# Value loads on another engine's queue, weight loads one piece less ahead, and a later start of the norm, in an attention and two-layer gated-FFN kernel

## The chip, the cores and the metric

One core of a Trainium2 chip runs the whole program. The metric is device time in microseconds (us), the median of several executions; the profile is one further execution with the hardware profiler on. Engines are named as the profile names them: PE is TensorE (PEld its weight loads), DVE VectorE, ACT ScalarE, POOL GpSimd, SP SyncE, which here only issues transfers ("SPq" in the trace).

## The reference

```python
def reference(q, k, v, w_a, w_b, w_out1, w_gate, w_val, w_out2, rms_g):
    # q, k, v: 4 batches, 8 heads, 576 tokens, 64 wide
    scores = q @ k.transpose(0, 1, 3, 2) / 8.0
    scores = where(block_of(i) >= block_of(j), scores, -1e9)     # blocks of 64 tokens
    attn = softmax(scores)
    x = (attn @ v).transpose(0, 2, 1, 3).reshape(2304, 512)
    x = ((x @ w_a) * (x @ w_b)) @ w_out1                          # 512 -> 1536 -> 512
    xn = x / sqrt(mean(x * x) + 1e-6) * rms_g
    g, val = xn @ w_gate, xn @ w_val
    return (g * sigmoid(g) * val) @ w_out2
```

## The kernel before, in words

The program has three parts that overlap. **Attention** (`attention`, L307 on) goes over 16 pairs of heads, numbered m = 0 to 15, four pairs to a batch. A pair is done in two halves of its rows (`part` 0 and 1), and step u = 2m + part scores one half, transposes the half before it and multiplies the half before that with the values. **Layer one** (`moe1`) follows batch by batch, in blocks of 512 or 1,024 tokens with 512 or 256 columns to a matmul. While it runs on one block, the attention of the next batch is woven in between its matmuls, so PE has work of two kinds in its queue. **Layer two** (`moe2`) has three blocks of 768 tokens and saves one product in eight twice over by sums of operands (seven products for eight, P1 to P7), 384 columns to a matmul. Nearly every operand of the layers is split in two, a rounded high part (made by ACT or DVE) and the rest (by DVE or POOL), and a product is three matmuls.

The kernel is written in an order, and a scheduler then sorts each engine's queue by its own estimates. Each engine then works off its queue strictly in order: an instruction that waits holds up all that stands behind it. Before the change every transfer is issued from SP's queue.

What the change touches:

- **The values.** `load_v(m)` (L387) fetches the values of pair m. The four pairs of the first batch (`WHOLE = 1`) are used whole. From pair 4 on they are split: `make_vv(m)` (L422) makes the high part at L114 and the rest at L429, both on POOL, from a raw tile `vr`. Pair 4 has a raw tile of its own; pairs 5 to 15 take turns in the two `vr` buffers, which pairs 0, 2 and 3 used before them, whole. So a load of the raw values waits until a former pair has read its buffer for the last time: for pair 5 these are the value matmuls of pair 2 on PE (L548), for most later pairs the split two pairs ahead on POOL (L429). Before, `load(m)`, called two pairs ahead, calls `load_v(m)`; each pair is two transfers of 160 KB, one for each head, at L403.
- **The weights.** Weights come as 8-byte numbers in 72 pieces of 512 KB. `prepare()` (L192) first lets `stage_loads` issue the loads of some pieces ahead (at L190), then decodes one piece: two ACT passes (L146, L149), a DVE shift (L152) and a POOL addition (L153), after which the piece is split (L111, L121) and written out again (L227). Five landing places go round (`LANDING = 5`: three in the tile `ld`, two in `st`). The load of a piece waits until the piece that lay in its place is decoded. Before, loads run up to five pieces ahead of the one decoded, for the first half of the pieces (layer one).
- **The norm.** `normed` (L1002) fetches the next block's tokens from DRAM (L1006), squares and sums them (L1009 and L1011 on ACT, L1012 on DVE), splits the sum, adds over partitions with two matmuls per half (L1023, L1024), takes the root and scales (L1026 to L1044), and `sums_of` makes four differences of operands (L959). `before_fc` (L1091) takes one step of it at each of the 24 calls in a block of layer two. Before, the first step is taken at the call with `fc` = 1.

At the border of the layers the tokens of the block after next have just been written to DRAM (L1088), and the norm's fetch of them waits for that write.

Of the kernel before, what the change touches and what calls it, by code (L numbers as in the profile page):

```python
# [16 lines left out]
P = 128  # L17
# [34 lines left out]
def tile_attention_moe_moe(  # L52
# [121 lines left out]
    def stage_loads(n):  # L174
        while len(staged) + prepared[0] < min(n, len(w_pieces)):
            i = len(staged) + prepared[0]
            layer, kind, f, y = w_pieces[i]
            if layer == 0 and i % LANDING < LANDING - 2:
                if not landing:
                    landing.append(stage.tile([P, LANDING - 2, 4 * P], I64, tag="bg", name="ld", bufs=1))  # L180
                st = landing[0][:, i % LANDING]
            else:
                st = stage.tile([P, 4 * P], I64, tag="st", name="st", bufs=2)
            if kind == "o" and layer == 1:

                for dm in range(KC):
                    z, o = divmod(dm * TF + f % TF, KC)
                    sp.dma_start(out=st[:, dm * P:dm * P + P], in_=w_o[1][f // TF, z, :, o * P:o * P + P])
            else:
                sp.dma_start(out=st, in_=(w_ab if kind == "ab" else w_o)[layer][f, y])  # L190
            staged[i] = st

    def prepare():

        i = prepared[0]
        if i >= len(w_pieces):
            return
        stage_loads(min(i + min(2 + i, LANDING), max(len(w_pieces) // 2, i + 2)))
        layer, kind, f, y = w_pieces[i]
        w = 4 * P  # L200
        if layer == 0:
            if y == 0:
                if kind == "ab":
                    wtiles["ab", f] = wab.tile([P, 4, KC * P], F32R, tag="ab", name="ab")
                else:
                    wtiles["o", f] = wop.tile([P, 2, TF * DM], F32R, tag="o", name="o")
            t = wtiles[kind, f]
            dst = t[:, 2 * y:2 * y + 2, :] if kind == "ab" else t[:, :, y * w:(y + 1) * w]
        else:
            if f % 2 == 0:  # L210
                quarters["src"] = stage.tile([P, 8, 2 * P], F32, tag="src", name="src", bufs=1)
            src = quarters["src"]
            if kind == "ab":
                at = (0, 6)[f % 2]
                place = src[:, at:at + 2, :]
            else:
                place = src[:, f % 2:f % 2 + 7:6, :]
            decode(staged.pop(i), place)
            prepared[0] += 1
            if f % 2 == 1:  # L220
                combine(wc_dram[f // 2][y] if kind == "ab" else wco_dram[f // 2], src)
            return
        x = decode(staged.pop(i)).rearrange("p a b -> p (a b)")
        prepared[0] += 1
        split(dst[:, 0, :], dst[:, 1, :], x, act, eng[W_LO[i % len(W_LO)]], "act")
        if y == (1 if kind == "ab" else TF - 1):
            sp.dma_start(out=wab_dram[f] if kind == "ab" else wo_dram[f], in_=t.bitcast(F32))  # L227
# [82 lines left out]
    def attention(pools, x_of, done):  # L310
# [44 lines left out]
        def load(m):  # L355
            if m >= NP:
                return
            b, h = divmod(m, H // 2)
            if single(m):
                t = k_raw[m] = ap2.tile([P, 2, S], F32, tag="kr", name="kr", bufs=1)  # L360
                for y in range(2):
                    rows = slice(y * D, y * D + D)
                    sp.dma_start(out=t[rows], in_=k[b, h].rearrange("(t d) s -> d t s", t=2))
                if m == FIRST_SINGLE:
                    load_q(m)
                load_v(m)
                return
            if m == 0:
                t = k_raw[m] = stage.tile([P, 8, 2 * P], F32, tag="src", name="src", bufs=1).rearrange(
                    "p a b -> p (a b)"  # L370
                )[:, 0:S]
            else:
                t = k_raw[m] = ap2.tile([P, 2, S], F32, tag="kr", name="kr", bufs=1)[:, 0]
                sp.dma_start(out=t, in_=k[b, h])
            for n0, n1 in ((0, FIRST), (FIRST, NQ)) if m == 0 else ((0, NQ),):
                cols = slice(n0 * Q, n1 * Q)
                if m == 0:
                    sp.dma_start(out=t[:, cols], in_=k[b, h][:, cols])
                for hh in range(2):
                    sp.dma_start(  # L380
                        out=qz[m % 2][hh * D:hh * D + D, n0:n1, hh, :],
                        in_=q[b, 2 * h + hh][:, cols].rearrange("d (n q) -> d n q", q=Q),
                    )
            if m > 1:
                load_v(m)

        def load_v(m):  # L387
            b, h = divmod(m, H // 2)
            if b < WHOLE:
                if m == 1:  # L390
                    t = ap2.tile([P, 2, NTILE, P], F32, tag="vv", name="vr")
                    t = vv[m] = t[:, 0].rearrange("p n (h d) -> p n h d", h=2)
                else:
                    t = vv[m] = ap2.tile([P, NTILE, 2, D], F32, tag="vr", name="vr")
                for hh in range(2):
                    sp.dma_start(out=t[:, :, hh], in_=v[b, 2 * h + hh])
                return
            if m == WHOLE * (H // 2):
                t = v_raw[m] = ap2.tile([P, 2, NTILE, P], F32, tag="vv", name="vr")[:, :, :, 0:D]
            else:  # L400
                t = v_raw[m] = ap2.tile([P, 2, NTILE, D], F32, tag="vr", name="vr")
            for hh in range(2):
                sp.dma_start(out=t[:, hh], in_=v[b, 2 * h + hh])  # L403

        def make_k(m):
            if m >= NP:
# [208 lines left out]
        for u in range(2 * NP + 2):  # L615
            m, part = divmod(u, 2)
            if u >= 2:
                yield from (whole_values if (u - 2) // H < WHOLE else values)(u - 2)
            sc = list(SCORED[part]) if m < NP else []
            ct = p_transposes(u - 1) if 1 <= u <= 2 * NP else iter(())  # L620
            if sc:
                yield score(m, sc.pop(0))
                if len(sc) > 2:
                    yield score(m, sc.pop(0))
                if part == 0:
                    make_vv(m)
                    make_q(m, 1)
                else:
                    make_k(m + 1)
                    if m + 1 > FIRST_SINGLE:  # L630
                        make_q(m + 1, 0)
            alive = True
            while sc or alive:
                c = next(ct, None) if alive else None
                if c is None:
                    alive = False
                else:
                    yield c
                if sc:
                    yield score(m, sc.pop(0))  # L640
            if m < NP and part == 1:
                if m + 1 == FIRST_SINGLE:
                    make_q(m + 1, 0)
                load(m + 2)
# [414 lines left out]
    for at, (layer, t0, n_tok, parts) in enumerate(blocks):  # L1059
# [32 lines left out]
        def before_fc(fc, n_tiles=n_tiles, at=at, layer=layer, following=following, norm=norm, got=got):  # L1092
            if at == 0:
                if fc > 0:
                    for _ in range(TF):
                        if prepared[0] < len(w_pieces) // 2:
                            prepare()
            elif layer == 0:
                if fc % TF == 0:
                    fetch_o(fc // TF)  # L1100
                if fc + 2 < FC:
                    fetch_ab(fc + 2)
                n = sum(BACKGROUND[:at]) + min(BACKGROUND[at], BACKGROUND[at] * (fc + 1) // (FC - 3))
                while prepared[0] < len(w_pieces) // 2 + n:
                    prepare()
                if prepared[0] == len(w_pieces) and not rings:
                    staging.close()
                    rings.append(ctx.enter_context(tc.tile_pool(name="ring", bufs=RING, side="right")))
                    fetch_to(RING - 1)
            if following and following[0] == 0 and fc + 2 >= FC:  # L1110
                fetch_ab(fc + 2 - FC)
            if fc > 0:
                for _ in range(FC * 2 // n_tiles):
                    if layer == 0 and len(got.get("x") or ()) == len(EARLY):
                        break
                    got["x"] = next(norm, None) or got.get("x")
# [100 lines left out]
```

## Time and profile before

| what | value |
|---|---|
| median of 3 runs | 1054.71 us (1053.46 to 1057.16) |
| the profiled execution: its time | 1053.99 us |
| its span on the core | 1052.0 us |
| granted TensorE clock, mean over the span | 0.998 |
| busy: PE, PEld | 1037.8 us (99%), 934.4 us (89%) |
| busy: DVE, ACT, POOL | 702.6 us, 619.0 us, 423.5 us |
| transfers | 281.25 MB, all but 1.08 MB of it from SP's queue |

A line of a timeline gives the start of an instruction and its duration in us, then engine, line, operation, tiles and shapes; in brackets the time for which the engine stood idle before it, and the instruction that ended that. A line of a waits view gives the instruction that waited, the one it waited for, and total us, number of times, longest us. The chain is the work that ended last, followed back in time: start, us, and what. PEclk is the granted TensorE clock as a share of full speed.

### The profile page before, as it was taken

What the parts mean: (1) busy time and instruction counts of PE and PEld (TensorE: products, weight loads), DVE (VectorE), ACT (ScalarE), POOL (GpSimd) and SP (SyncE); (2) the same over time, 40 slices, a digit from 0 to 9 for tenths busy, and PEclk for the clock granted to TensorE, in tenths of its full rate; (3) what the DMA queues carried; (4) which work ended last, traced back from release to release, by engine and by line L of the source; (5) the groups of instructions that cost most, each with busy time, mean ns of one, the idle gap of its engine ahead of it and who ended that gap; (6) DMA issues with size and microseconds to landing.
All of it is one profiled execution on the core that took longest, in us unless ns stands there. A gap on an engine that the chain in (4) does not pass through costs nothing.

```text
span 1052.0 us, 16959 instructions
## 1 busy us (share of the span) xinstructions
PE 1037.8 (99%) x5676; PEld 934.4 (89%) x5676; DVE 702.6 (67%) x1371; ACT 619.0 (59%) x1376; POOL 423.5 (40%) x448
## 2 busy tenths in 40 slices
PE   9989999999999999999999999999999999999998
PEld 6768877899998888888888888999999999999998
DVE  5546767677766777676687734784876838666285
ACT  7868968667656766556544323653656536355362
POOL 5855766546564655455554501120221202212020
PEclk9999999999999999999999999999999999999999
DMA  9865978889997765788989665787789888887883
GB/s 242 232 202 194 294 258 300 313 270 290 347 371 261 270 223 210 288 330 313 340 312 349 255 225 181 216 284 258 242 301 302 275 268 251 294 265 240 266 247 116
DMA packets 116380, 281.25 MB, mean 267 GB/s; under 512 B 27971, under 2 KB 40771, under 8 KB 105798
## 3 DMA queue, kind: packets, MB, share of 16 engines
q1 hardware_dynamic: 116294, 280.18, 79.8%
q8 instruction: 45, 0.74, 0.3%
q14 instruction: 41, 0.34, 0.1%
HBM read 218.77 MB, written 61.36 MB: 266 GB/s over the span
## 4 chain that ended last, share of the span: by engine, by line
PE 85%; ACT 4%; DMA 4%; DVE 2%; POOL 2%; SPq 1%; issue 1%; POOLq 0%; ACTq 0%
PE mm L735 25%; PE mm L766 12%; PE mm L707 8%; PE mm L708 8%; PE mm L709 8%; PE mm L667 4%; PE mm L668 4%; PE mm L669 4%; PE t L592 3%; PE t L523 3%; PE s L465 3%; PE t L548 1%; DMA st<-in_w_o_dram 1%; POOL x L153 1%; PE s L457 1%
## 5 line engine op out<-in xcount | busy, mean ns | idle before, releaser
L708 PE MATMUL mm<-xl,ab 128*128 128x512 f32 (+1 forms) x480 | 180.8, 377 | 0.0
L707 PE MATMUL mm<-xh,ab 128*128 128x512 f32 (+1 forms) x480 | 179.8, 377 | 0.0
L709 PE MATMUL mm<-xh,ab 128*128 128x512 f32 (+1 forms) x480 | 179.4, 374 | 0.0
L735 PE MATMUL mm<-hT,w 128*128 128x384 f32 x576 | 165.5, 337 | 1.3 <-ACT mm L743 1.3
L121 POOL TENSOR_TENSOR hl<-g,hh 128x384 fp32r<-128x384 f32 x36 | 42.7, 1186 | 298.7 <-ACT hh L111 298.7
L735 PE MATMUL mm<-hB,w 128*128 128x384 f32 x432 | 125.9, 336 | 0.0
L766 PE MATMUL mm<-hh,w 128*128 128x384 f32 x504 | 125.2, 336 | 0.0
L743 ACT ACTIVATE mm<-mm 128x384 f32<-128x384 f32 x144 | 66.8, 474 | 75.5 <-PE mm L735 39.3
L735 PEld LDWEIGHTS mm<-hT,w 128*128 128x128 f32 x576 | 105.9, 188 | 2.7 <-ACT mm L743 2.4
L709 PEld LDWEIGHTS mm<-xh,ab 128*128 128x128 f32 x480 | 90.5, 189 | 15.2 <-issue 0.5
L707 PEld LDWEIGHTS mm<-xh,ab 128*128 128x128 f32 x480 | 90.4, 188 | 15.1 <-issue 0.2
L708 PEld LDWEIGHTS mm<-xl,ab 128*128 128x128 f32 x480 | 90.5, 189 | 14.8 <-issue 0.2
L498 POOL TENSOR_SCALAR pp<-pp,st 128x256 f32<-128x256 f32 (+4 forms) x144 | 83.3, 592 | 50.0 <-DVE st L495 35.5
L735 PE MATMUL mm<-lT,w 128*128 128x384 f32 x288 | 96.9, 337 | 0.0
L486 ACT ACTIVATE pp<-s,st 128x288 f32<-128x288 f32 (+8 forms) x142 | 72.0, 510 | 33.0 <-DVE st L480 16.2
L766 PEld LDWEIGHTS mm<-hh,w 128*128 128x128 f32 x504 | 90.6, 188 | 0.3 <-ACT mm L743 0.3
L766 PE MATMUL mm<-hl,w 128*128 128x384 f32 x252 | 81.4, 336 | 0.0
L735 PEld LDWEIGHTS mm<-hB,w 128*128 128x128 f32 x432 | 79.5, 188 | 0.0
L667 PE MATMUL mm<-hh,o 128*128 128x512 f32 (+1 forms) x208 | 77.8, 375 | 1.2 <-DVE acc L677 0.7
L153 POOL TENSOR_TENSOR src<-src,st 128x512 uint32<-128x512 uint32 x36 | 47.8, 1328 | 74.0 <-DVE src L152 74.0
L668 PE MATMUL mm<-hh,o 128*128 128x512 f32 (+1 forms) x208 | 77.4, 373 | 0.0
L669 PE MATMUL mm<-hl,o 128*128 128x512 f32 (+1 forms) x208 | 75.3, 370 | 0.4 <-DVE hl L121 0.4
(161 smaller groups left out, 2453.4 us busy)
## 6 DMA issues: line engine op xcount, KB each, us to landing
w<-wc SPq DMA_DIRECT2D x252, 256.0 KB, 3.5
ab<-wab SPq DMA_DIRECT2D x36, 1024.0 KB, 7.9
w<-wco SPq DMA_DIRECT2D x126, 256.0 KB, 3.3
wc<-bg SPq DMA_DIRECT2D x12, 1792.0 KB, 8.3
o<-wo SPq DMA_DIRECT2D x12, 1536.0 KB, 8.0
st<-in_w_ab_dram SPq DMA_DIRECT2D x34, 512.0 KB, 5.7
wab<-ab SPq DMA_DIRECT2D x12, 1024.0 KB, 5.9
wco<-bg SPq DMA_DIRECT2D x6, 1792.0 KB, 6.6
```

Source lines behind the costliest of these rows:

```text
L153: pool.tensor_tensor(x, x, lo, ALU.add)
L486: act.activation(pi[:, a:z], pss[x][:, 0:z - a], AF.Exp, bias=s[:, b:b + 1], scale=1.0, accum_out=t3[:, b, x:x + 1],)
L498: pool.tensor_scalar(t, t, s[:, y:y + 1], 1.0, ALU.mult, ALU.mult)
L667: pe.matmul(ps[:, 0:n], wh, hh, start=(y == 0), stop=False)
L668: pe.matmul(ps[:, 0:n], wl, hh, start=False, stop=False)
L669: pe.matmul(ps[:, 0:n], wh, hl, start=False, stop=(y == TF - 1))
L707: pe.matmul(ps[:, 0:n], wh[:, a:z], xhc, start=(c == 0), stop=False)
L708: pe.matmul(ps[:, 0:n], wh[:, a:z], xlc, start=False, stop=False)
L709: pe.matmul(ps[:, 0:n], wl[:, a:z], xhc, start=False, stop=(c == KC - 1))
L735: pe.matmul(ps, lhs, rhs[:, c, :], start=(start and c == 0 and y == 0), stop=(c == 1 and y == 2), skip_group_check=not start,)
L743: act.activation(to, ps, AF.Copy)
L766: pe.matmul(banks[m], lhs, rhs, start=(start and f == group[0] and y == 0), stop=(f == group[-1] and y == 2), skip_group_check=not start,)
```

## The change

Values of pairs 5 to 15 are loaded by one transfer of 320 KB each from POOL's queue, and the load for pair m + 1 is written directly behind the split of pair m. Weight loads run four pieces ahead where they ran five ahead. In layer two the norm's first step is taken at the call with `fc` = 3; layer one's calls (`layer` = 0) are as they were.

```diff
@@ prepare
-        stage_loads(min(i + min(2 + i, LANDING), max(len(w_pieces) // 2, i + 2)))
+        stage_loads(min(i + min(2 + i, LANDING - 1), max(len(w_pieces) // 2, i + 2)))
@@ load
                 if m == FIRST_SINGLE:
                     load_q(m)
-                load_v(m)
                 return
...
-            if m > 1:
+            if 1 < m <= WHOLE * (H // 2):
                 load_v(m)
@@ load_v
             if m == WHOLE * (H // 2):
                 t = v_raw[m] = ap2.tile([P, 2, NTILE, P], F32, tag="vv", name="vr")[:, :, :, 0:D]
-            else:
-                t = v_raw[m] = ap2.tile([P, 2, NTILE, D], F32, tag="vr", name="vr")
-            for hh in range(2):
-                sp.dma_start(out=t[:, hh], in_=v[b, 2 * h + hh])
+                for hh in range(2):
+                    sp.dma_start(out=t[:, hh], in_=v[b, 2 * h + hh])
+                return
+            t = v_raw[m] = ap2.tile([P, 2, NTILE, D], F32, tag="vr", name="vr")
+            pool.dma_start(out=t, in_=v[b, 2 * h:2 * h + 2].rearrange("t p n d -> p t n d"))
@@ attention, part 0 of pair m
                     make_vv(m)
+                    if WHOLE * (H // 2) <= m < NP - 1:
+                        load_v(m + 1)
                     make_q(m, 1)
@@ before_fc
-            if fc > 0:
+            if fc > 2 * layer:
```

How this moves instructions in the queues, at the three places the prediction speaks of. (Line numbers of the changed kernel are higher by one or two from `make_vv` on.)

**POOL, around the split of pair 5.** L153 decodes weights, L498 scales a tile `pp` of softmax rows, L114 and L429 split the values of pair 5, and L121 is a split of weights. Before:

```order
L153 TENSOR_TENSOR x<-x,ld 128x512
L498 TENSOR_SCALAR pp_158<-pp_158,st 128x576
L114 TENSOR_SCALAR vv<-vr 128x10x64
L429 TENSOR_TENSOR vv<-vr,vv 128x10x64
L153 TENSOR_TENSOR x<-x,ld 128x512
L498 TENSOR_SCALAR pp_156<-pp_156,st 128x448
L498 TENSOR_SCALAR pp_157<-pp_157,st 128x512
L121 TENSOR_TENSOR o<-x,o 128x512
```

Now:

```order
L153 TENSOR_TENSOR x<-x,ld 128x512
L498 TENSOR_SCALAR pp_158<-pp_158,st 128x576
L403 DMA vr<-in_v_dram 128x2x320
L114 TENSOR_SCALAR vv<-vr 128x10x64
L429 TENSOR_TENSOR vv<-vr,vv 128x10x64
L153 TENSOR_TENSOR x<-x,ld 128x512
L498 TENSOR_SCALAR pp_156<-pp_156,st 128x448
L498 TENSOR_SCALAR pp_157<-pp_157,st 128x512
L403 DMA vr<-in_v_dram 128x2x320
L121 TENSOR_TENSOR o<-x,o 128x512
```

The load of pair 5 (the first L403) stands right in front of the split that needs it, and the load of pair 6 four rows behind that split; on SP the two pairs of L403 rows are gone and its other rows stand in the order they had.

**ACT, at the border of the layers.** L111 makes high parts of layer two's first operands, L1009 and L1011 are the norm's squares, L743 and L862 copy products out of PSUM for PE. Before:

```order
L111 ACTIVATE hT_6896<-T_6522 128x768
L1009 ACTIVATE sq<-xf 128x768
L1011 ACTIVATE y<-xf 128x768
L743 ACTIVATE mm<-mm 128x384
L1011 ACTIVATE y<-xf 128x768
L862 ACTIVATE p_7042<-mm 128x384
L743 ACTIVATE mm<-mm 128x384 x2
L1011 ACTIVATE y<-xf 128x768
L819 ACT_TABLE_LOAD
```

Now (L1013 was L1011, L745 was L743, L864 was L862, L821 was L819):

```order
L111 ACTIVATE hT_6885<-T_6511 128x768
L1013 ACTIVATE y<-xf 128x768
L745 ACTIVATE mm<-mm 128x384
L864 ACTIVATE p_7031<-mm 128x384
L745 ACTIVATE mm<-mm 128x384 x2
L821 ACT_TABLE_LOAD
```

One of the two squares that stood in front of the first PSUM copy is still there; the other, and two more, have moved some ten rows back.

**ACT, in the later attention of layer one.** L486 are exponentials of scores, L146 and L149 decode weights, and L111 splits them. Before:

```order
L146 ACTIVATE ld<-ld 128x512
L149 ACTIVATE a<-ld 128x512
L486 ACTIVATE pp_154,st<-s,st 128x320
L111 ACTIVATE ab<-x 128x512
L486 ACTIVATE pp_155,st<-s,st 128x384
L597 ACTIVATE xf<-t 64x192
L111 ACTIVATE o<-x 128x512
```

Now:

```order
L146 ACTIVATE ld<-ld 128x512
L111 ACTIVATE ab<-x 128x512
L486 ACTIVATE pp_154,st<-s,st 128x320
L149 ACTIVATE a<-ld 128x512
L486 ACTIVATE pp_155,st<-s,st 128x384
L111 ACTIVATE ab<-x 128x512
L597 ACTIVATE xf<-t 64x192 x2
```

The second exponential stands ahead of the split of weights that was between the two; swaps of this kind fill the stretch on ACT, DVE, POOL and PE.

## Rows read from the trace of the kernel before

**Rows 1.** The page's 40 slices: PE's clock, in tenths.

```profile
PEclk9999999999999999999999999999999999999999
```

**Rows 2.** Waits of PE from 50 us to the end: seven of all eight rows.

```profile
PE t L523 <- POOL pp L498: 3.2, 4, 2.0
PE mm L735 <- ACT mm L743: 1.3, 1, 1.3
PE s L457 <- ACT pp L486: 1.1, 1, 1.1
PE mm L667 <- DVE acc L677: 0.7, 2, 0.4
PE t L592 <- DVE pl L529: 0.5, 1, 0.5
PE mm L667 <- ACT hh L111: 0.5, 1, 0.5
...
PE mm L669 <- DVE hl L121: 0.4, 1, 0.4
```

**Rows 3.** Timeline of POOL, 56 to 66 us.

```profile
56.31 0.74 POOL L498 TENSOR_SCALAR pp<-pp,st 128x576 f32<-128x576 f32 x1
61.36 0.72 POOL L114 TENSOR_SCALAR vv<-vr 128x640 fp32r<-128x640 f32 x1 [4.31 <-DMA vr<-in_v_dram]
62.17 1.55 POOL L429 TENSOR_TENSOR vv<-vr,vv 128x640 fp32r<-128x640 f32 x1
```

**Rows 4.** Timeline of PE, 56 us: the value matmuls of pair 2.

```profile
56.10 0.39 PE L548 MATMUL t<-pw,vr 128*128 128x128 f32 x2
```

**Rows 5.** Timeline of SP's queue, 56 us: the row before the load.

```profile
56.35 0.33 SPq L190 DMA_DIRECT2D ld<-in_w_o_dram  x1
```

**Rows 6.** The chain: the load of pair 5, eleven transposes soon after, and eleven later.

```profile
57.21 4.00 DMA vr<-in_v_dram
...
67.05 2.35 PE t L523 x11
...
196.61 1.20 PE t L523 x11
```

**Rows 7.** Windows: stretch, PE, PEld, DVE, ACT, POOL, then PEclk, DMA share, GB/s.

```profile
67.00:68.00 1.00, 1.00 (x7) 1.00 (x6) 0.42 (x1) 0.28 (x1) 0.47 (x1) 0.50 0.84 344
...
250.00:275.00 25.00, 25.00 (x208) 24.83 (x207) 21.08 (x59) 19.44 (x52) 17.25 (x21) 1.00 1.01 345
```

**Rows 8.** Line L403, all 24 transfers: from issue to landing, us.

```profile
DMA to landing us min/median/max: 2.2/3.4/9.4
```

**Rows 9.** Timeline of POOL: what follows the places of the next five value loads.

```profile
69.36 1.51 POOL L498 TENSOR_SCALAR pp<-pp,st 128x64 f32<-128x64 f32 x4 [1.89 <-DVE st L495]
77.43 1.29 POOL L121 TENSOR_TENSOR xl<-xf,xh 128x512 fp32r<-128x512 f32 x1 [2.87 <-DVE xh L113]
111.23 1.31 POOL L153 TENSOR_TENSOR x<-x,ld 128x512 uint32<-128x512 uint32 x1 [0.37 <-DVE x L152]
146.91 0.75 POOL L498 TENSOR_SCALAR pp<-pp,st 128x576 f32<-128x576 f32 x1 [3.01 <-ACT ph L525]
182.92 0.75 POOL L498 TENSOR_SCALAR pp<-pp,st 128x576 f32<-128x576 f32 x1 [1.10 <-DVE st L495]
```

**Rows 10.** Waits of PE, 110 to 215 us: two of four; the others stand above.

```profile
PE t L523 <- POOL pp L498: 1.2, 3, 0.6
...
PE mm L667 <- DVE acc L677: 0.3, 1, 0.3
```

**Rows 11.** The chain at the border of the layers.

```profile
644.02 7.70 DMA xf<-x_dram
...
651.74 0.02 ACT sq L1009
...
652.49 0.82 ACT y L1011
```

**Rows 12.** Timeline of DVE, 59 us: the last of four operations that follow each other.

```profile
59.29 0.69 DVE L121 TENSOR_TENSOR xl<-xf,xh 128x512 fp32r<-128x512 f32 x1 [0.33 <-ACT xh L111]
```

## The prediction

> **What bounds the kernel now.** I read the page's slices first: PE's clock is at its full level in every slice [rows 1], and the table above has PE busy for 99% of the span. So PE is the bound, and a change can give back only what PE loses. The waits of PE come second [rows 2]. From 50 us to the end they are 3.2 + 1.3 + 1.1 + 0.7 + 0.5 + 0.5 + 0.4 + 0.4 = 8.1 us (the row left out is one of the two of 0.4). Beside the waits there is one stretch near 67 us at half clock, granted 0.50 [rows 7]: eleven transposes took 2.35 us there, against 1.20 later [rows 6], so 1.15 lost. That is 9.3 us of 1,054 in all; no version of this change can bring 1%.
>
> The two largest waits lie where the diff works, so I read their surroundings third. The first is the 2.0 us at L523, which waits for a `pp` of POOL's. POOL was late because it had stood idle for 4.31 us before the split of pair 5's values, L114 at 61.36, until their load landed [rows 3]. That load runs on the chain from 57.21 to 61.21 [rows 6]. PE idles, and right behind it comes the half clock. The second is the 1.3 us at L735 at the border of the layers: ACT first makes two squares of the norm and only then the copy of PSUM for which PE waits [rows 2, 11].
>
> **The change part by part.**
>
> *A, the load of pair 5.* It leaves SP's queue and stands on POOL's between the scale L498 and the split. Does it start earlier? Its buffer is free when PE is through with pair 2's values, at 56.10 + 0.39 = 56.49 [rows 4]; SP was at another load until 56.35 + 0.33 = 56.68 [rows 5], so SP lost nothing by standing elsewhere. POOL comes to the load when L498 ends, at 56.31 + 0.74 = 57.05 [rows 3], later than SP. The buffer is free by then, so the load adds no wait on a semaphore; but the next row on POOL needs its data, so all of its landing is again POOL's idle time. No row of this kernel shows a load issued by POOL. For POOL's hold I have below the 0.33 of an issue on SP [rows 5], above the 1.55 of L429, POOL's longer pass over the same tile [rows 3]. I take 1.14, the mean of its two passes over that tile, 0.72 and 1.55, since the tile is the same, though a descriptor is no pass. For landing I keep the 4.00 of this load. Then L114 begins at 57.05 + 1.14 + 4.00 = 62.19 where it began at 61.36: **+0.83**. From below: hold 0 and the shortest landing of this line, 2.2 [rows 8], give 59.25, 2.11 earlier; PE's wait of 2.0 goes with it. From above: hold 1.55 and the longest landing, 9.4, give 68.0, 6.6 later.
>
> *B, the other ten loads.* Each holds POOL for 1.14. The next five stand ahead of idle times of POOL of 1.89, 2.87, 0.37, 3.01 and 1.10 [rows 9], so four of the five are covered to within 0.04 and one runs over by 0.77, in front of a decoding addition, L153, not of something PE waits for. The last ones fall where PE works through without a gap, 25.00 of 25 [rows 7]. I take **0**; without that cover, +0.8. They land in time: the places are 8 to 36 us apart, the median landing 3.4 [rows 8, 9].
>
> *C, SP without the loads, and four pieces ahead.* SP's remaining rows stand in the order they had, and a piece's load starts when its place is decoded, which the count of pieces ahead doesn't alter: **0**. If the count did bite, PE would wait for weights, of which there is no row now [rows 2].
>
> *D, the re-sorted stretch from 110 to 215 us.* PE waits 1.2 + 0.3 [rows 10] and, in the same stretch, 1.1 and 0.5 of the rows above (L457 and L667 behind `hh`) [rows 2]: 3.1 in all. It can lose at most that and, by the same measure, gain as much again. The one readable move is that exponentials pass ahead of splits of weights, and L457 waits for an exponential; I take half of its 1.1: **-0.55**.
>
> *E, the norm.* At the border one of the two squares leaves the place ahead of L743, which comes 652.49 - 651.74 = 0.75 sooner [rows 11]: **-0.75** of PE's 1.3. The other square stays and waits for the 7.70 us fetch as before, so the wait isn't gone. Bounds: 0, if the square that stays carries the whole wait, and -1.3. In the later blocks the norm begins two calls later, under cover of the rest of the block. If that cover were gone, PE would stand at each of two borders about as at this one, +2.6.
>
> Sum: 0.83 + 0 + 0 - 0.55 - 0.75 = -0.47, so 1053.99 becomes 1053.5 in an execution like the profiled one; the median of the runs is 0.72 above that one, so **1054.2**.
>
> **The rivals.**
>
> *Faster, 0.22.* The 4.00 of pair 5's load is not its own time: SP issued a 512 KB load right ahead of it [rows 5], which at 345 GB/s [rows 7] takes 1.5 us of the same transfer engines. On a queue of its own, and in one piece, it may land in the shortest 2.2 [rows 8], and POOL's hold may lie inside the landing. Then L114 comes 2.11 earlier, PE's wait of 1.98 to 2.0 goes, and without the gap the 1.15 of half clock: -2.0 - 1.15 - 0.75 - 0.55 = -4.45, or **1050.3**. Against it: the 512 KB are under way whatever queue the values come from. The Trainium skill's page "DMA: Bandwidth & Descriptors", section "Anatomy of one DMA — SWDGE (gpsimd) path", fits 2.0 us plus bytes over 436,000 to a transfer from GpSimd; for 320 KB I estimate 2.75 us from it, L114 at 59.8, and a gain of most of the 2.0. By that rule this rival holds; no run here shows such a load yet.
>
> *Slower, 0.12.* Loads issued by POOL are held up while DVE works. Behind 57.05 DVE is busy almost without a break until 59.29 + 0.69 = 59.98 [rows 12]: a hold of 2.93 in place of 1.14. Pair 5 then lands at 63.98, +2.62, and the same hold at the next five places runs over the idle times there by 1.04 + 0.06 + 2.56 + 0 + 1.83 = 5.5 [rows 9]. If all of that came through to PE: +2.62 + 5.5 - 0.75 - 0.55 = +6.8, **1061.5**. It decides from a hold of about 2 us on, where POOL's idle times no longer cover it. For it: POOL's splits and scales stand right behind the loads. Against it: most of POOL's lateness before 215 us ends in PE's queue of other work, which now lets through only 8.1 us in all. The Trainium skill has this mechanism on the page "SBUF — State Buffer", section "SBUF: two separate sides": descriptors of GpSimd's transfers can't be written while DVE holds the shared port in some of its copies; a transfer of 620 ns took some 3,100 beside one. Only some operations of DVE do it by that page, and no row here shows one that does.
>
> *The re-sorted stretch costs, 0.06.* D is +3.1 where I took -0.55: **1057.9**.
>
> *The norm comes too late, 0.04.* E's cover is gone: +2.6, **1056.8**.
>
> That the change doesn't do what it says is true of one part, the four pieces ahead (C), and lies inside the forecast.
>
> **How the numbers follow.** About 0.3%, 3.2 us here, can be told from no change. The forecast has 0.56; its own bounds reach from -2.1 to +6.6 for A alone, so I leave 0.05 of it to each side. Faster: 0.05 + 0.20 of the first rival (its 4.45 is over 3.2) = 0.25. Slower: 0.05 + 0.12 + 0.03 of the re-sorted stretch + 0.02 of the norm, rounded, = 0.22. The rest, 0.53, is no difference. The range takes in the first rival, 1050.3, with 0.8 below it for a landing still shorter or more of D, and the re-sorted stretch and A's hold at its upper end above, up to 1059.0; it leaves out the slower rival and the outermost bounds of A and D.
>
> **What would show it.** Right: POOL's L114 of pair 5 at about 62.2, one wait of PE of some 2 to 3 us for a `pp` soon after it, half clock behind that, and L735's wait at the border down from 1.3 to about 0.55. The first rival: L114 before 60, no long wait of PE there, no slice at half clock near 67. The slower rival: POOL standing over 2 us at each L403, and new waits of PE for POOL's `pp` or `vv` from 66 to 190 us. The prediction is wrong if PE's waits grow or shrink by more than 3 us at a place not named here, above all from 110 to 215 us, or if weights appear among what PE waits for.

## The result, and the profile after

The changed kernel takes **1066.33 us**, the median of 6 runs (1064.32 to 1070.28), against 1054.56 for the kernel before, measured beside it. The ratio is 1.0103 with a 95% interval of 1.0076 to 1.0130: slower by 8 to 14 us. The profiled execution spans 1062.6 us (1052.0 before); the granted clock is 0.995 over the span (0.998 before).

PE's waits from 50 us to the end, in the waits view of the changed kernel (total us, times, longest):

```profile
PE t L523 <- POOL pp L498: 3.0, 1, 3.0
PE mm L768 <- ACT hh L111: 2.1, 1, 2.1
PE mm L737 <- ACT mm L745: 2.0, 3, 1.1
PE s L457 <- ACT pp L486: 1.8, 1, 1.8
PE s L465 <- ACT pp L486: 1.7, 1, 1.7
PE mm L669 <- DVE acc L679: 1.5, 2, 1.1
PE mm L768 <- ACT mm L745: 0.8, 2, 0.6
```

With three more rows (0.5, 0.4, 0.4) they come to 14.2 us, where [rows 2] has 8.1. L735 and L766 of before are L737 and L768 here. To see where they fall, I took the time at which PE has done the same amount of matmul columns in both traces; the difference is what the changed kernel is behind at that point of the work. It is good to about 0.3 us where the two do their work in another order:

| place, us of before | behind at its end, us | of it made there |
|---|---|---|
| 0 to 34 (the start) | -0.5 | -0.5 |
| 60 to 87 (pair 5's values) | +0.5 | +1.0 |
| 87 to 207 | -0.5 | -1.0 |
| 207 to 230 | +3.2 | **+3.7** |
| 230 to 646 | +3.2 | 0.0 |
| 646 to 663 (layer border) | +2.7 | -0.5 |
| 693 to 708 (first block of layer two) | +7.1 | **+4.4** |
| 800 to 845 (second block) | +10.4 | **+3.3** |
| 845 to 1041 | +10.1 | -0.3 |

So there are three losses, and the largest is the norm's, inside the blocks of layer two, where the forecast had put it at nothing.

**Pair 5's values.** Timeline of POOL at the place of [rows 3], and PE's wait behind it:

```profile
55.79 0.74 POOL L498 TENSOR_SCALAR pp<-pp,st 128x576 f32<-128x576 f32 x1
56.48 0.91 POOL L403 DMA_DIRECT2D vr<-in_v_dram  x1
61.91 0.72 POOL L114 TENSOR_SCALAR vv<-vr 128x640 fp32r<-128x640 f32 x1 [4.52 <-DMA vr<-in_v_dram]
```

```profile
66.14 0.33 PE L523 MATMUL t<-ident,pp 128*128 128x128 f32 x1 [3.00 <-POOL pp L498]
```

The issue holds POOL for 0.91, then POOL stands for 4.52 until the data are there, 4.31 in [rows 3]. PE's wait is 3.0 where it was 2.0.

**The stretch from 207 to 230 us.** ACT's timeline, before and now: the high part of q stands for its load, and behind it stand the exponentials that PE's L465 waits for.

```profile
211.18 0.53 ACT L111 ACTIVATE qh<-qr 128x384 fp32r<-128x384 f32 x1 [2.39 <-POOL pp L498]
...
213.79 0.94 ACT L111 ACTIVATE qh<-qr 128x384 fp32r<-128x384 f32 x2 [4.75 <-DMA qr<-in_q_dram]
```

In the trace of before the view names a scale of POOL's, which ended at 211.08; q landed at that moment too, so even there it had no time to spare. The line of q's two loads, before and now (from issue to landing, us):

```profile
DMA to landing us min/median/max: 10.7/11.1/11.5
...
DMA to landing us min/median/max: 14.0/14.3/14.5
```

Two timelines of SP's queue show what stands ahead of q's load, L345. Before:

```profile
187.06 0.33 SPq L190 DMA_DIRECT2D st<-in_w_ab_dram  x1
187.44 0.42 SPq L254 DMA_DIRECT2D o<-wo  x1
...
191.52 0.33 SPq L190 DMA_DIRECT2D st<-in_w_ab_dram  x1
194.25 0.33 SPq L250 DMA_DIRECT2D ab<-wab  x1
195.50 0.33 SPq L227 DMA_DIRECT2D wab<-ab  x1
196.06 0.32 SPq L227 DMA_DIRECT2D wo<-o  x1
198.95 1.53 SPq L345 DMA_DIRECT2D qr<-in_q_dram  x2
```

Now:

```profile
186.75 2.64 SPq L190 DMA_DIRECT2D st<-in_w_ab_dram  x2
189.49 0.38 SPq L254 DMA_DIRECT2D o<-wo  x1
...
192.36 0.53 SPq L227 DMA_DIRECT2D wab<-ab  x1
195.85 0.33 SPq L227 DMA_DIRECT2D wo<-o  x1
196.27 0.57 SPq L250 DMA_DIRECT2D ab<-wab  x1
198.53 1.27 SPq L345 DMA_DIRECT2D qr<-in_q_dram  x2
```

The rows are the same, their order is not: two of them have moved. The second L190 now stands ahead of the fetch L254 (1.5 MB) and holds the queue for some 2 us until its landing place is free; the fetch L250 (1 MB) now stands behind the two stores L227 and goes out 2 us later, right in front of q. From about 190 us on the transfer engines are full (a DMA share of 0.9 or more in every 2 us up to 214 before, up to 216 now), and q lands 14 us after its issue, where it was 11. Whether what is queued ahead of q does that is tried below.

**Layer two.** At the border PE's wait of 1.3 [rows 2] is shorter:

```profile
656.22 0.44 PE L737 MATMUL mm<-hT,w 128*128 128x384 f32 x1 [0.57 <-ACT mm L745]
```

Inside the blocks it is otherwise. DVE's timeline, the first scaling of the norm in the first and second block, and PE's wait in the first:

```profile
701.29 1.02 DVE L1046 SCALAR_TENSOR_TENSOR xf<-xf,rms_g,y 128x768 f32<-128x768 f32 x1 [2.65 <-DMA y<-row]
...
839.33 1.02 DVE L1046 SCALAR_TENSOR_TENSOR xf<-xf,rms_g,y 128x768 f32<-128x768 f32 x1 [3.63 <-DMA y<-row]
```

```profile
705.38 1.65 PE L768 MATMUL mm<-hh,w 128*128 128x384 f32 x4 [2.06 <-ACT hh L111]
```

DVE stands for `y`, the row of factors that goes out to DRAM and comes back spread over the partitions. Behind that scaling in DVE's queue are the gating operations (L883, L888, L828) from which ACT makes `hh`, and PE runs dry of `hh`. In the trace of before the scaling has no idle time in front of it:

```profile
687.78 1.93 DVE L1044 SCALAR_TENSOR_TENSOR xf<-xf,rms_g,y 128x768 f32<-128x768 f32 x2
```

The windows view shows that the clock pays too (columns as in [rows 7]; the rows of before at the same work, 698 to 708 us, have 5.00 and a clock of 1.00):

```profile
700.00:705.00 5.00, 3.32 (x20) 3.00 (x18) 3.68 (x7) 0.72 (x2) 0.95 (x2) 1.00 1.02 364
705.00:710.00 5.00, 4.62 (x17) 4.62 (x18) 5.00 (x7) 2.45 (x6) 1.63 (x2) 0.66 0.63 191
```

### The profile page after: what moved, and what is told of

It reads as the page before. It is cut to its first block, busy times and chain, and to the rows that moved or that the text cites. A ratio compares the mean times of both kernels' runs of the same rounds, so it can differ in the third digit from the quotient of the medians.

```text
span 1062.6 us, 16966 instructions
## 1 busy us (share of the span) xinstructions
PE 1042.0 (98%) x5676; PEld 937.5 (88%) x5676; DVE 706.8 (67%) x1371; ACT 619.1 (58%) x1376; POOL 428.9 (40%) x459
## 4 chain that ended last, share of the span: by engine, by line
PE 78%; ACT 6%; DVE 5%; DMA 5%; POOL 3%; issue 2%; SPq 0%; POOLq 0%; ACTq 0%; DVEq 0%
PE mm L737 22%; PE mm L768 11%; PE mm L709 8%; PE mm L710 8%; PE mm L711 8%; PE mm L669 4%; PE mm L670 4%; PE mm L671 4%; PE t L592 3%; PE t L523 3%; PE s L465 2%; DMA qr<-in_q_dram 2%; POOL x L153 1%; PE t L548 1%; ACT pp L486 1%
## 5 line engine op out<-in xcount | busy, mean ns | idle before, releaser
L737 PE MATMUL mm<-hT,w 128*128 128x384 f32 x576 | 165.4, 338 | 2.2 <-ACT mm L745 2.0
L121 POOL TENSOR_TENSOR hl<-g,hh 128x384 fp32r<-128x384 f32 x36 | 41.7, 1158 | 298.7 <-ACT hh L111 298.7
L768 PE MATMUL mm<-hh,w 128*128 128x384 f32 x504 | 127.6, 340 | 2.9 <-ACT hh L111 2.1
L737 PE MATMUL mm<-hB,w 128*128 128x384 f32 x432 | 125.4, 336 | 0.0
L745 ACT ACTIVATE mm<-mm 128x384 f32<-128x384 f32 x144 | 67.1, 474 | 82.2 <-PE mm L737 48.6
L737 PEld LDWEIGHTS mm<-hT,w 128*128 128x128 f32 x576 | 105.9, 188 | 4.4 <-ACT mm L745 4.0
L498 POOL TENSOR_SCALAR pp<-pp,st 128x256 f32<-128x256 f32 (+4 forms) x144 | 82.4, 585 | 52.9 <-DVE st L495 39.2
L737 PE MATMUL mm<-lT,w 128*128 128x384 f32 x288 | 96.9, 337 | 0.0
L768 PEld LDWEIGHTS mm<-hh,w 128*128 128x128 f32 x504 | 91.8, 190 | 4.0 <-ACT hh L111 2.4
L486 ACT ACTIVATE pp<-s,st 128x288 f32<-128x288 f32 (+8 forms) x142 | 72.1, 512 | 34.8 <-DVE st L484 16.0
L768 PE MATMUL mm<-hl,w 128*128 128x384 f32 x252 | 82.5, 338 | 0.0
L737 PEld LDWEIGHTS mm<-hB,w 128*128 128x128 f32 x432 | 79.5, 188 | 0.0
L153 POOL TENSOR_TENSOR src<-src,st 128x512 uint32<-128x512 uint32 x36 | 47.9, 1329 | 74.0 <-DVE src L152 72.7
```

The lines of the kernel that those rows point to most:

```text
L153: pool.tensor_tensor(x, x, lo, ALU.add)
L486: act.activation(pi[:, a:z], pss[x][:, 0:z - a], AF.Exp, bias=s[:, b:b + 1], scale=1.0, accum_out=t3[:, b, x:x + 1],)
L498: pool.tensor_scalar(t, t, s[:, y:y + 1], 1.0, ALU.mult, ALU.mult)
L737: pe.matmul(ps, lhs, rhs[:, c, :], start=(start and c == 0 and y == 0), stop=(c == 1 and y == 2), skip_group_check=not start,)
L745: act.activation(to, ps, AF.Copy)
L768: pe.matmul(banks[m], lhs, rhs, start=(start and f == group[0] and y == 0), stop=(f == group[-1] and y == 2), skip_group_check=not start,)
```

## The experiments

### Each part alone

`norm_only` and `four_only` are the kernel before with one line of the change each, `loads_only` is the kernel before with the diff's other lines (in `load`, `load_v` and `attention`), and `no_norm` is the changed kernel without the line of `norm_only`.

```diff
# norm_only
-            if fc > 0:
+            if fc > 2 * layer:
# four_only
-        stage_loads(min(i + min(2 + i, LANDING), max(len(w_pieces) // 2, i + 2)))
+        stage_loads(min(i + min(2 + i, LANDING - 1), max(len(w_pieces) // 2, i + 2)))
```

> The kernel before, with only the norm's first step at the call with fc = 3 in layer two. If the losses in layer two come from the later norm alone (DVE standing at the scaling, L1044 here, for the row y): the border gains 0.5, the first two blocks of layer two lose 4.4 and 3.1, in all +6.9, about 1061.5, and DVE idles 2 to 4 us before the first scaling of each block. Rival, that the loss needs the new order of the loads as well: within 1 us of before.

Measured: 1062.62 us, ratio 1.0068 (1.0045 to 1.0092), +7 us. DVE's rows of the two scalings:

```profile
699.17 1.02 DVE L1044 SCALAR_TENSOR_TENSOR xf<-xf,rms_g,y 128x768 f32<-128x768 f32 x1 [4.39 <-DMA y<-row]
...
837.81 1.02 DVE L1044 SCALAR_TENSOR_TENSOR xf<-xf,rms_g,y 128x768 f32<-128x768 f32 x1 [4.20 <-DMA y<-row]
```

The later norm loses this without the loads; the rival is out. In the profile the border gains 0.6 us, and the two blocks lose 6.3 and 4.1.

> The changed kernel with the norm's first step back at fc = 1. If the norm alone makes the losses of layer two: +3.2 against before, about 1057.8, with all of the difference made before 235 us (pair 5's values +1.0, the stretch from 110 to 235 us +2.7, minus the 0.5 that the start differs). Rival, that layer two loses for another reason: still 7 us more behind 690 us.

Measured: 1059.12 us, ratio 1.0046 (1.0031 to 1.0060), +4.9. Layer two loses next to nothing (0.4 us in the profile); the early losses are larger than expected, 1.6 at pair 5 and 3.8 from 207 to 230 us.

> The kernel before, with only the values of pairs 5 to 15 loaded from POOL's queue behind the split of the pair ahead; five pieces ahead and the norm as before. If the loads alone make the early losses: PE's wait for pair 5's rows 3.0 where it was 2.0, the same order from 110 to 235 us as in the changed kernel, +3.2, about 1057.8. Rival, that four pieces ahead brings weights and with them the loads of q later: only pair 5's +1.0, about 1055.7.

Measured: 1059.28 us, ratio 1.0042 (1.0023 to 1.0061). PE waits 3.5 at L523 for POOL and 1.9 at L465, and ACT takes q at 214.6: the whole early loss without the four pieces ahead. All queues have the same order as in `no_norm`.

> The kernel before, with only the weight loads four pieces ahead. If the place that is freed sets the load and not the count: within 0.5 us of before, 1054.7. Rival, that four ahead is what delays the stretch from 200 to 230 us: +2 to +3.

Measured: 1054.39 us, ratio 0.9994 (0.9976 to 1.0012): nothing, and no row of any queue stands elsewhere than before. The two losing parts, 1.0068 and 1.0042, add up to 1.0110, within the noise of the change's 1.0103.

### What the later norm waits for

`norm_y4` is the changed kernel, `norm_only_y4` the kernel before with the later norm, each with

```diff
         behind(sp.dma_start(out=y, in_=row[1, :].partition_broadcast(P)), "gate")
-        for _ in range(3):
+        for _ in range(4):
             yield None
```

> The changed kernel with one more empty step of the norm between the fetch of the row y and the first scaling, which puts that scaling behind the products of a group's second half. If DVE's wait for y is what layer two loses: 7 to 8 us less than the changed kernel, about 1058.5, with no idle time of DVE before the scaling. Rival, that the later norm costs by its other work (table loads, sums and splits pressed together): less than half of it comes back, over 1062.

Measured: 1063.01 us, ratio 1.0065 (1.0041 to 1.0088). DVE no longer stands for `y`, but by the ratios only some 4 us came back, and 1063 is the rival's number. The total of the profiled execution is no clear witness: against the changed kernel it loses 3.6 us between 20 and 25 us, where the program is the changed kernel's own. But from 693 us on it falls only 3.4 us further behind the kernel before, where the changed kernel falls 7.4; 2.4 of the 3.4 are lost in the second block.

> The kernel before with the later norm and that one empty step more, and nothing else of the change. By the first theory only the gain at the border is left: 0.5 to 1.2 less than before, about 1053.7. By the rival: 3 us or more above before.

Measured: 1056.45 us, ratio 1.0018 (1.0004 to 1.0031): some 5 of 7 us back, not all. Most of the rest, 2.8 us in the profile, is lost at one place, in the second block. ACT, then PE:

```profile
819.24 0.21 ACT L1031 ACTIVATE sm<-sm 128x6 f32<-128x6 f32 x1 [0.91 <-DMA sm<-row]
```

```profile
819.88 0.44 PE L735 MATMUL mm<-hT,w 128*128 128x384 f32 x1 [0.73 <-ACT mm L743]
823.33 0.44 PE L735 MATMUL mm<-hT,w 128*128 128x384 f32 x1 [1.07 <-ACT mm L743]
```

So there is a second wait of the same kind: the root stands on ACT for the row of sums on its way through DRAM, with the copy that PE needs behind it. `norm_only_sq` puts the empty step there instead:

```diff
+        yield None
         behind(act.activation(r, v, AF.Sqrt), "hh")
```

> The kernel before with the later norm, and the empty step not ahead of the scaling but between the fetch of the row of sums and the root (L1031). If what the later norm loses is two waits in queues, DVE's for y at the scaling and ACT's for the sums at the root near 819 us: both go, and what is left is the border's gain, 0.5 to 1 below before, about 1054. Rival, that the root is no part of it: as the version with the step ahead of the scaling, 1.8 above before.

Measured: 1055.19 us, ratio 1.0002 (0.9986 to 1.0018). Root and scaling now have next to no idle time in front of them (0.43 at one scaling), and the loss is gone. Between the fetch of `y` and the scaling there are three calls here too, as in the kernel before and in `norm_only`; what differs is the time between them. In the first block DVE comes to the scaling 9.0 us after the fetch is issued in the kernel before, 1.5 us after it in `norm_only` and 4.8 in `norm_only_sq`, and the fetch takes 4 to 6 us to land. The border's half a microsecond is below what the runs can tell.

### What POOL's loads cost

`place_sp` is `no_norm` with the same single transfer at the same place of the program, from SP:

```diff
-            pool.dma_start(out=t, in_=v[b, 2 * h:2 * h + 2].rearrange("t p n d -> p t n d"))
+            sp.dma_start(out=t, in_=v[b, 2 * h:2 * h + 2].rearrange("t p n d -> p t n d"))
```

> The changed kernel with the norm's start as before and the values loaded at the new place in the program, but from SP's queue. There SP's queue again has the weight fetch L250 ahead of the two weight stores, and the loads of q behind them. If the late q of 213 us comes from that fetch standing right ahead of q: the loss from 205 to 230 us is gone, and pair 5's load starts as before, so within 1 us of before. Rival, that the place in the program and the order on PE and ACT make it: still +3 to +4.

Measured: 1054.57 us, ratio 1.0002 (0.9987 to 1.0017). ACT's step and the order on SP are those of before again:

```profile
210.75 0.52 ACT L111 ACTIVATE qh<-qr 128x384 fp32r<-128x384 f32 x1 [2.44 <-DMA qr<-in_q_dram]
```

It is the move to POOL's queue that costs, not the new place in the program. Two versions of `no_norm` move a single row of SP's; every other row of every queue stands where it stood. `q_first` has q's load ahead of L250 (the fetch is written one call later, by lines of `before_fc` left out here, and held behind q); `o_first` has L254 ahead of the second L190:

```diff
# q_first, load_q
-                sp.dma_start(out=t[y * D:y * D + D], in_=q[b, 2 * h:2 * h + 2].rearrange("t d s -> d t s"))
+                gate["q"] = sp.dma_start(out=t[y * D:y * D + D], in_=q[b, 2 * h:2 * h + 2].rearrange("t d s -> d t s"))
# q_first, fetch_ab
-        sp.dma_start(out=t.bitcast(F32), in_=wab_dram[n])
+        d = sp.dma_start(out=t.bitcast(F32), in_=wab_dram[n])
+        if n == 0 and prepared[0] == 36 and "ab0" not in gate:
+            gate["ab0"] = d
+            behind(d, "q")
# o_first, stage_loads (d is the load of piece i, o0 the first fetch_o)
+                if i == 37:
+                    behind(d, "o0")
```

> The changed kernel with the norm's start as before, and on SP's queue the load of q at 199 us ahead of the weight fetch L250 instead of behind it; no other row of any queue differs. If the fetch ahead makes q late: q lands 2 to 3 us earlier, PE's wait of 1.9 at L465 goes, 2 to 3 us less than without the swap, about 1056.5. Rival, that q waits for what was queued long before: same landing, about 1059.

Measured: 1056.56 us, ratio 1.0020 (1.0011 to 1.0030). ACT takes q at 210.99 without a wait for it (215.34 in `no_norm`), and PE's wait at L465 is not in the waits view any more.

> The changed kernel with the norm's start as before, and on SP's queue the fetch L254 (1.5 MB) ahead of the second of two weight loads at 187 to 189 us, as it was before. If the hold of SP's queue by that weight load (2.3 us) makes all that follows late: q lands 2 us earlier and 2 to 3 us come back, about 1056.5. Rival, that the fetch L250 alone does it: about 1059.

Measured: 1056.87 us, ratio 1.0018 (1.0006 to 1.0029); ACT takes q at 212.4. In both profiles the loss between 207 and 224 us is 0.7 where `no_norm` has 3.8. So q is late because of what stands ahead of it on SP, and moving one of the two rows is enough; both at once were not tried. Of the 2 us that are left, 0.7 to 1.0 are pair 5's in these profiles and 0.7 are lost here.

`q_pool` sends q's load through POOL's queue too:

```diff
-                sp.dma_start(out=t[y * D:y * D + D], in_=q[b, 2 * h:2 * h + 2].rearrange("t d s -> d t s"))
+                pool.dma_start(out=t[y * D:y * D + D], in_=q[b, 2 * h:2 * h + 2].rearrange("t d s -> d t s"))
```

> The changed kernel with the norm's start as before, and the loads of q (L345) from POOL's queue as well. If q waits behind a weight fetch on SP's queue: q lands within 6 us of its issue at 200 us, PE's wait at L465 goes, and 2.5 to 4 of the 4.7 us come back, about 1056. Rival, that the transfers share the engines whatever the queue: q lands as late as before, about 1059 or more.

Measured: 1060.70 us, ratio 1.0036 (1.0013 to 1.0060). q's two halves land 9.3 and 11.2 us after their issues at 199.8 and 200.5 (14.1 and 14.6 in `no_norm`), so another queue passes part of the traffic and not all of it; ACT takes q at 211.8, the wait at L465 is gone, and 3 us with it. But the order moves again, and PE now waits for weights:

```profile
297.72 0.35 PE L709 MATMUL mm<-xh,ab 128*128 128x256 f32 x1 [3.11 <-DMA ab<-wab]
```

In the profile 4.7 us are lost here. The total is the rival's, 1059 or more (five of the seven runs lie between 1059 and 1063, two near 1056), but not by the rival's reason: q came earlier, and the loss moved to another place.

### Pair 5, and a version that beats both

`split_later` (in the kernel before) and `loads_split_later` (in `no_norm`) hold the split of pair 5 behind the two scales for which PE waits, and `split_later_sq` is `split_later` with the later norm of `norm_only_sq`. The hold does more than its text says: the scheduler then sorts every queue anew from 61 us on (ACT's rows alone differ in order at over 100 places from the kernel without the hold), so what these versions gain or lose elsewhere is not the hold's own.

```diff
-                        pool.tensor_scalar(t, t, s[:, y:y + 1], 1.0, ALU.mult, ALU.mult)
+                        gate["pp", m] = pool.tensor_scalar(t, t, s[:, y:y + 1], 1.0, ALU.mult, ALU.mult)
...
-            copy(pool, hi, t)
+            hi_made = copy(pool, hi, t)
+            if m == 5:
+                behind(hi_made, ("pp", 3))
```

> The kernel before, with the split of pair 5's values held behind the two scales (448 and 512 wide) for which PE waits; nothing of the change. If PE's wait of 2.0 and the half clock behind it come from POOL standing for pair 5's load: the wait goes, the clock stays full near 67 us, 2 to 3.1 us less, about 1052. Rival, that PE then waits at the values themselves, near 76 us: within 1 us of before.

Measured: 1053.27 us, ratio 0.9980 (0.9953 to 1.0006): not clear of no change. The profile says why. Near 65 us the wait and the half clock are gone, and PE is 3.4 us ahead at 87 us, which is the repair. By 207 us it is 8.4 ahead; the further 5 come from the new order: the waits of 3.1 us that the kernel before has in that stretch [rows 2, 10] are gone, and the rest is not traced to a row. Then it gives 5.4 back within 10 us, waiting for q, with the clock falling; in this execution the rest and 3 us more go near 300 us, where PE also waits 1.8 for a weight fetch. The windows:

```profile
65.00:70.00 5.00, 5.00 (x23) 3.42 (x22) 1.88 (x5) 3.85 (x10) 4.88 (x7) 1.00 0.40 137
205.00:210.00 5.00, 2.02 (x9) 1.62 (x8) 0.92 (x3) 3.17 (x12) 2.57 (x4) 0.77 0.81 317
210.00:215.00 5.00, 5.00 (x15) 4.08 (x15) 3.74 (x11) 2.32 (x9) 3.99 (x9) 0.55 0.17 63
```

> Both of the two versions before in one. If the gains add: 3 to 4 us below before, about 1051. Rival: no better than the better one of the two alone.

Measured: 1051.82 us, ratio 0.9976 (0.9957 to 0.9996), about what the split alone gives. In its profile PE is ahead by 7.2 us at 207 us and by 1.2 at 216.

> The changed kernel with the norm's start as before, and the split of pair 5 held behind the two scales. Of the 4.7 us that POOL's loads cost, the part at pair 5 (1.0 to 1.5 over before, and the 2.0 to 3.1 that before loses there itself) goes; the late q near 213 us stays: 3 to 4.5 below the version without the hold, about 1055. Rival, that the new order makes the loss everywhere: 1058 or more.

Measured: 1054.47 us, ratio 0.9994 (0.9980 to 1.0008), by the ratios some 5 us below `no_norm`. The total is the expected one, but not by the expected places. PE is 3.7 us ahead of the kernel before at 87 us and still 3.4 at 230 us, so the late q near 213 us did not stay. The lead goes between 280 and 290 us instead, where ACT stands 4.25 for q. So the total equals that of the kernel before because the gain at pair 5 is lost again elsewhere; it does not show that the loads on POOL cost nothing. The rival, a loss everywhere, is out.

`q_first_sum` adds to `split_later_sq` the one moved row of `q_first`, the fetch L250 behind q; no other row of any queue differs:

> The version with the later split of pair 5 and the later root, and q ahead of the fetch L250. If its loss at 213 us is q's landing behind 1 MB: 2.5 to 3 us of the 6 lost there come back, about 1049. Rival, that the fetch is then late for PE (a wait of L709 for ab appears): no gain, about 1052.

Measured: **1047.04 us, ratio 0.9936 (0.9917 to 0.9956)**, some 7 us faster than the kernel before and 19 faster than the changed one. The lead of 8 us survives 216 us and lasts to the end; all waits of PE from 50 us on come to 3.1 us. The windows at the place where the two versions before lost theirs:

```profile
205.00:210.00 5.00, 5.00 (x28) 4.26 (x27) 4.35 (x11) 2.79 (x11) 4.13 (x10) 1.00 0.72 285
210.00:215.00 5.00, 5.00 (x32) 4.46 (x31) 4.44 (x8) 4.10 (x9) 1.59 (x3) 1.00 0.51 165
```

By the ratios that is some 4 us below `split_later_sq`, more than the 2.5 to 3 expected of the move.

`all_three` puts the same three repairs into the whole changed kernel:

> The whole changed kernel with the root one call later, the split of pair 5 behind the two scales, and q ahead of the fetch L250. If the three places are all that it loses: within 2 us of the same three repairs in the kernel before, about 1047 to 1049. Rival, that the loads on POOL cost more than these places: 1052 or more.

Measured: 1053.33 us, ratio 0.9993 (0.9982 to 1.0004). The rival's bound (1052 or more) is met: the three repairs undo the change's loss but bring nothing over before. Against `q_first_sum` it falls behind by 4 us between 152 and 172 us, and by 3 near 281, where ACT again stands for q:

```profile
281.60 0.52 ACT L111 ACTIVATE qh<-qr 128x384 fp32r<-128x384 f32 x1 [3.84 <-DMA qr<-in_q_dram]
```

With the loads on POOL the queues have another order in both stretches. There PE waits 1.3 for an exponential (L486 of before) and 1.3 for `hh`. Which row is to blame was not tried, so what the loads on POOL cost in this order, some 6 us by the ratios, is measured but its cause is open.

## Why the prediction was wrong

The forecast was no change, 1054.2, in a range up to 1059.0; the time lies 7 us above the range.

- **E, the norm, failed.** The border came out as said: PE's wait there is 0.57 where 0.55 was forecast, and the gain 0.5 where 0.75 stood. The sentence "In the later blocks the norm begins two calls later, under cover of the rest of the block" was the wrong step. It looked only at the norm's end, and asked what was late for the next block. The norm is a chain with two round trips through DRAM (sums out and in, factors out and in), and between the trips its steps stand in the queues of engines on which PE depends. Two calls later, the steps that wait for a trip stood too near behind it: 4.4 + 3.3 us inside the blocks, where the forecast had 0. The rival on the norm had the right part of the kernel and the wrong mechanism and price (+2.6, at the borders), with a chance of 0.04. `norm_only_sq` shows that one empty step ahead of the root undoes it.
- **C failed in one sentence.** "SP's remaining rows stand in the order they had" holds for all but three rows of layer one, and two of the three count: near 187 to 199 us the second L190 and the fetch L250 moved, q came 3 us later, and 3.7 us were lost where the forecast had 0. That four pieces ahead cost nothing was right (0.9994).
- **D was wrong in its mechanism and its sign.** It took half of L457's wait of 1.1 as gained; that wait grew to 1.8, while the other waits of the stretch, 2.0 in all, went. Up to 207 us the changed kernel gained 1.0 and `no_norm`, whose queues have the same order there, 0.1, so the 0.55 is not shown. Within D's own stretch, which ends at 215 us, q's lateness begins: PE is 1.9 behind at 216 us where it was 0.5 behind at 110. The rival on this stretch (+3.1) had nearly the place and the price, but the cause was SP's order, not the new order on ACT and PE.
- **A was right**, in mechanism and size: POOL needs 5.43 from the issue to the split (61.91 - 56.48), where 1.14 + 4.00 = 5.14 was taken, and PE falls behind by 1.0 where 0.83 was forecast (0.7 to 1.8 in the other profiles with this order). The two terms were off in opposite directions: the hold was 0.91 and not 1.14, the wait for the data behind it 4.52 and not 4.00. The faster rival is out: the load on its own queue took 5.3 us to land, not 2.2. The Trainium skill's page "DMA: Bandwidth & Descriptors", section "Anatomy of one DMA — SWDGE (gpsimd) path", has a fit from which the estimate for this size was 2.75; the trace does not agree with it: here the eleven loads took 3.3 to 10.0, beside other traffic.
- **B was right, and the slower rival is out.** All eleven issues on POOL, from the view of line L403 (ns, min/median/max):

```profile
L403 POOL DMA_DIRECT2D vr<-in_v_dram x11: 758/763/906, 56.5 to 329.6; - x11
```

No hold comes near 2 us, nor in the other runs with these loads (0.91 at most), and none shows a load of POOL's held up by DVE.
- The statement that all that PE loses is 8.1 us of waits and 1.15 of clock was a sound bound for gains (`q_first_sum` got 7), but it says nothing of losses: steps that cause no wait can still have nothing to spare, as q, which landed in the kernel before at the moment when the scale that ACT also waited for was done.

## What to carry to other kernels

When a chain of small steps with trips through DRAM is moved, check each step that waits for a trip, on its own engine's queue: what stands behind it, and by how much the data beat it before. When transfers leave a queue, compare that queue's whole order before and after, not only around the rows removed: here, with the transfer engines full, moving one row (a fetch of 1 MB behind q, or one of 1.5 MB ahead of the load that held the queue) was worth some 3 us to what stood behind it. A wait taken away pays only as far as the next transfer that sets the pace; here the lead of 8 us came to the end only when the load of q was moved forward too. And where a scheduler sorts the queues, a small hold is not a small experiment: compare the whole order before a gain is put down to it.

## What was not expected of the hardware

A load issued from POOL held POOL for only 0.76 to 0.91 us, less than the 1.14 that the passes over the same tile had suggested. And in a stretch with full transfer engines, q on POOL's queue landed 9.3 and 11.2 us after its issues, hardly sooner than from SP's queue in the kernel before (10.7 and 11.5), though on its own queue no weight fetch stood ahead of it.
